# Two sets of float32 buffers for the slot weights, and a fixed order of a slot's work on TensorE, VectorE and ScalarE

## The chip, the cores and the metric

The kernel runs on one core of one Trainium2 chip. The metric is the time of one execution in microseconds (us), as the device reports it. Lower is better.

## What is computed

Three layers in a chain: linear attention, a SoLU feed-forward layer, and a top-1 routed mixture of experts.

```python
k_s = softmax(k, axis=seq); q_s = softmax(q)              # (8, 8, 576, 64)
x = q_s @ (k_s^T @ v)                                     # -> 4608 tokens x 512
h = x @ w_in                                              # 512 x 1024
x = layernorm(h * softmax(h)) * g_ln @ w_out              # 1024 x 512
e_idx = argmax(x @ w_gate + modality_bias[modality_id])   # 8 experts
for e in range(8):                                        # w1 512 x 1024, w2 1024 x 512, float32
    mask = e_idx == e
    out[mask] = gate_w[mask] * (relu(x[mask] @ w1[e]) @ w2[e])
```

All inputs are float32. Products of float32 are made as three float16 products (high by high, high by low, low by high), so each weight is split into a high and a low part at a scale that is a power of two.

## The kernel before

**Stages.** First come the attention sums, then 36 tiles of 128 tokens pass through attention and the SoLU layer (the tile stage, lines 480 to 820; `ph` is the first product, `lnT` the transposed activations that a DMA brings, `px` the second product). Each tile also routes its tokens. From about 544 us on the routed layer runs in slots: a slot is 256 tokens of one expert. Eighteen slots are always there (`NMIN`), the rest is done in half slots by `tail` (L1328).

**One slot.** `slot_load_w` (L929) loads the expert's weights on SP's queue: `w1` in four DMAs of 512 KB (L938) into `raw1`, `w2` in four (L941) into `raw2`. There is one such pair of float32 buffers, and from slot 1 on a load carries a condition, so that nothing is moved when the slot's expert is that of the slot before:

```python
g["kw"] = {} if i == 0 else {"cond": ld(i, 2, 1)}
SY.dma_start(out=raw1[:, c, :], in_=w1[ds(g["e"], 1), ...], **g["kw"])
```

`slot_split` (L948) makes the float16 pairs `w1b[i % 2]` and `w2b[i % 2]`: `mx` takes maxima of `w1` on DVE (L956, four), `l1` row sums of `w2` on ACT (L960, four, whose other output goes into a part of `w2b` that is written later). `fin` (L963) makes the scales from them: exponents on DVE (L102, L103), diagonals `dg` (L113), a product `pm` on PE (L115), a maximum `p2m` over it (L117), the scale `sc` (L123) and its inverse (L125, L967). Then `sp1` and `sp2` write the high part on ACT (L149) and the low part on DVE (L156), four pieces each for `w1b` and `w2b`.

`slot_gather` (L997) fetches the slot's tokens: their indices `six` (L1004, a small DMA on SP), two gathers of 128 rows into `sg` (L1009, issued by POOL), and two DMA transposes into `sxt` (L1013, on SP).

`slot_mm` (L1069) computes: `st1` on PE, two halves of 48 products `sph` (L1090); `ev1` after each half, `rl` and the high part of `hh` on ACT (L1097, L1098), the low part on DVE (L1099); `st2`, two halves of 24 products `spo` (L1108); `ev2` on ACT, `ob` (L1119), and a scatter of 128 rows to the output (L1022, issued by POOL).

**What sets the order.** Work is put into a queue by `at(time, fn)` (L64), and `flush` emits it in order of these times, which the loop at L1318 writes out by hand. `behind` (L70) holds a piece back behind a marked instruction, and `ordered` (L1062) keeps PE's products in the order of emission. For the rest a list scheduler (`TC_KW`, L37), which works from a cost model, orders the instructions of each engine. The loop body for slot i:

```python
mm(i, b)
if i:
    slot_gather(i + 1, b + 0.5)
    split(i + 1, b)
slot_load_w(i + 2, b + 18.0, 0.01)
```

So while PE does slot i, the weights of slot i + 1 are measured, scaled and split, and the load for slot i + 2 follows.

Of the kernel before, what the change touches and what calls it, by code (L numbers as in the profile page):

```python
# [43 lines left out]
def tile_attn_moe_moe(ctx, tc, q, kT, v, w_in, w_out, g_ln, mod, w_gate, bias, w1, w2, out):  # L44
# [884 lines left out]
    def slot_load_w(i, time, dt):  # L929
        g = {}  # L930

        def regs():
            g["e"] = ld(i, 1, NE - 1)
            g["kw"] = {} if i == 0 else {"cond": ld(i, 2, 1)}

        def one(r, c):
            if r == 1:
                SY.dma_start(out=raw1[:, c, :], in_=w1[ds(g["e"], 1), c * 128:(c + 1) * 128, :].rearrange(  # L938
                    "o p f -> (o p) f"), **g["kw"])
            else:  # L940
# [127 lines left out]

    def slot_mm(i, times):  # L1069
# [5 lines left out]
        def st1(k):  # L1075
            ordered(st1_, k)

        def st2(k):
            ordered(st2_, k)

        def st1_(k):
# [3 lines left out]
            for ff in range(4):  # L1085
                f = 4 * k + ff
                n = 0
                for c in range(4):
# [4 lines left out]

        def ev1(k):
# [3 lines left out]
            A.activation(out=g["hh"][:, 0, sl, :], in_=rl, func=AF.Copy)  # L1098
            V.tensor_tensor(out=g["hh"][:, 1, sl, :], in0=rl, in1=g["hh"][:, 0, sl, :], op=ALU.subtract)  # L1099

        def st2_(k):
            if k == 0:
# [2 lines left out]
            for h in range(2):
                for f in range(4 * k, 4 * k + 4):
                    for a, b2 in ((0, 0), (0, 1), (1, 0)):
                        last_mm[:] = [T.matmul(po[:, h, :], hh[:, a, f, h * 128:(h + 1) * 128], s2[:, b2, f, 0:DM],  # L1108
                                               start=(f == 0 and (a, b2) == (0, 0)), stop=(f == 7 and a == 1))]
# [7 lines left out]
        def ev2(h):  # L1117
# [1 line left out]
            A.activation(out=ob, in_=g["po"][:, h, :], func=AF.Copy, scale=g["rs"][:, h:h + 1])  # L1119
# [268 lines left out]
```

## Time and profile before

| | |
|---|---|
| time, median of 3 runs | 995.01 us (992.31 to 995.11) |
| the profiled execution | 994.26 us |
| its span, first to last instruction | 992.5 us |
| mean granted clock of TensorE | 0.968 |
| PE busy | 871.6 us (88%) |
| DVE, ACT, POOL busy | 779.0 (78%), 696.8 (70%), 475.5 (48%) us |
| DMA, mean over the span | 135 GB/s |

The profile is of one execution. PE is TensorE, DVE VectorE, ACT ScalarE, POOL GpSimd, SP the engine whose queue issues most DMAs. Busy times are sums over the whole span; the stages differ. A wait stands in square brackets behind an instruction, with what released it. A transfer's issue has a row on the queue's engine; the transfer itself is seen only in the DMA share and in who waits for it.

### The profile page before, as it was taken

To read this page: it belongs to the slowest core of one execution; us is meant where nothing else is said; L and a number is where in the kernel's file an instruction comes from. 1 tells how busy PE (TensorE), PEld (TensorE's weight loads), DVE (VectorE), ACT (ScalarE), POOL (GpSimd) and SP (SyncE) were. 2 spreads that over 40 slices of the span, in tenths; PEclk is the share of its full clock that TensorE was granted. 3 is DMA by queue.
4 is the path that set the end of the run, shared out by engine and by line. 5 is a ranking of instruction groups with operands and counts; after the bars stand their busy time and mean duration, and the time that the engine had idled before them with its cause. 6 is when DMAs were issued, how large, how long until landed. Compare 5 with 4: busy or idle time off the path is not lost.

```text
span 992.5 us, 18881 instructions
## 1 busy us (share of the span) xinstructions
PE 871.6 (88%) x6566; PEld 584.8 (59%) x6566; DVE 779.0 (78%) x1591; ACT 696.8 (70%) x1041; POOL 475.5 (48%) x892
## 2 busy tenths in 40 slices
PE   2476898999999998999996989999998999999983
PEld 1244666667676665766765755666665566666552
DVE  6979687887888868886897588888887877778871
ACT  5568677777876867675783657777768777777771
POOL 6734568777787776665656331222322222222221
PEclk9977999999999999999997998999999999999997
DMA  9959969787978687677445332222263223332360
GB/s 313 310 128 194 231 142 192 162 172 148 203 156 184 143 159 192 138 188 185 83 107 108 70 78 55 66 65 65 76 195 115 65 65 79 81 78 65 102 198 25
DMA packets 247483, 133.52 MB, mean 135 GB/s; under 512 B 215441, under 2 KB 218065, under 8 KB 247378
## 3 DMA queue, kind: packets, MB, share of 16 engines
q1 hardware_dynamic: 239938, 112.20, 50.3%
q0 software_dynamic: 7152, 20.01, 6.5%
q8 instruction: 53, 0.87, 0.4%
q14 instruction: 52, 0.43, 0.1%
q10 hardware_dynamic: 288, 0.02, 0.0%
HBM read 130.94 MB, written 19.86 MB: 152 GB/s over the span
## 4 chain that ended last, share of the span: by engine, by line
DVE 39%; PE 21%; issue 11%; ACT 10%; DMA 9%; POOL 7%; SPq 1%; ACTq 0%; POOLq 0%; DVEq 0%
PE spo L1108 9%; DVE w1b L156 8%; DVE w2b L156 7%; DVE smm L956 6%; PE px L710 4%; PE ph L596 3%; ACT w1b L149 2%; DVE vhl L156 2%; PE sph L1090 2%; DVE hh L1099 2%; DVE zhl L648 2%; ACT e L619 2%; DMA raw<-in_v_dram 2%; DVE t L625 1%; PE pk L502 1%
## 5 line engine op out<-in xcount | busy, mean ns | idle before, releaser
L710 PE MATMUL px<-w2b,lnT 128*128 128x256 f16 x1728 | 207.6, 277 | 12.2 <-DMA lnT<-zhl 12.2
L1090 PE MATMUL sph<-sxt,w1b 128*128 128x256 f16 x1728 | 199.3, 274 | 14.3 <-DVE w1b L156 11.5
L1108 PE MATMUL spo<-w2b,hh 128*128 128x512 f16 x864 | 194.6, 379 | 11.6 <-DVE hh L1099 9.8
L596 PE MATMUL ph<-w1b,xTt 128*128 128x512 f16 x864 | 198.6, 384 | 3.0 <-ACT xTt L149 3.0
L1090 PEld LDWEIGHTS <-w1b 128*128 128x128 f16 x1728 | 166.9, 98 | 47.5 <-DVE w1b L156 20.7
L710 PEld LDWEIGHTS <-lnT 128*128 128x128 f16 x1728 | 167.8, 99 | 40.0 <-DMA lnT<-zhl 13.2
L1108 PEld LDWEIGHTS <-hh 128*128 128x128 f16 x864 | 82.7, 98 | 112.8 <-DVE hh L1099 18.4
L596 PEld LDWEIGHTS <-xTt 128*128 128x128 f16 x864 | 84.4, 99 | 97.7 <-issue 5.1
L1022 POOL DMA_INDIRECT out_dram<-ob,six x37 | 59.1, 1597 | 151.3 <-ACT ob L1119 141.5
L149 ACT ACTIVATE w1b<-raw,sc 128x1024 f16<-128x1024 f32 x76 | 81.2, 1137 | 63.3 <-DVE sc L123 63.3
L156 DVE SCALAR_TENSOR_TENSOR w1b<-raw,sc,w1b 128x1024 f16<-128x1024 f32 x76 | 93.0, 1279 | 15.9 <-ACT w1b L149 15.9
L156 DVE SCALAR_TENSOR_TENSOR w2b<-raw,sc,w2b 128x1024 f16<-128x1024 f32 x76 | 95.3, 1275 | 0.0
L956 DVE TENSOR_REDUCE smm<-raw 128x1 f32<-128x1024 f32 x76 | 91.8, 1210 | 0.9 <-DMA raw<-in_moe_w_dram 0.9
L1009 POOL DMA_INDIRECT sg<-xs_scr,six x38 | 37.7, 991 | 107.3 <-issue 77.3
L960 ACT ACTIVATE w2b<-raw 128x1024 f16<-128x1024 f32 x76 | 79.4, 1046 | 7.9 <-DMA raw<-in_moe_w_dram 7.9
L149 ACT ACTIVATE w2b<-raw,sc 128x1024 f16<-128x1024 f32 x76 | 81.0, 1134 | 0.0
L648 DVE TENSOR_TENSOR zhl<-e,zhl 128x1024 f16<-128x1024 f32 x36 | 59.8, 1664 | 17.9 <-ACT zhl L645 15.1
L630 ACT ACTIVATE e<-t,hts 128x1024 f32<-128x1024 f32 x36 | 41.2, 1145 | 25.6 <-DVE t L625 25.4
L619 ACT ACTIVATE e<-ph,hnm,ghb 128x1024 f32<-128x1024 f32 x32 | 38.4, 1200 | 26.8 <-DVE hnm L615 23.7
L530 POOL TENSOR_TENSOR qr<-qr,qmx 128x512 f32<-128x512 f32 x36 | 38.9, 1084 | 33.2 <-DVE qmx L529 24.4
L643 ACT ACTIVATE e<-t,hna,ha 128x1024 f32<-128x1024 f32 x36 | 44.3, 1232 | 14.7 <-DVE hna L640 7.1
L625 DVE SCALAR_TENSOR_TENSOR t<-ph,ghb,e 128x1024 f32<-128x1024 f32 x32 | 41.0, 1281 | 15.1 <-ACT e L619 14.9
(263 smaller groups left out, 1434.6 us busy)
## 6 DMA issues: line engine op xcount, KB each, us to landing
raw<-in_moe_w_dram SPq DMA_DIRECT2D x160, 512.0 KB
qr<-in_q_dram SPq DMA_DIRECT2D x36, 256.0 KB
xs_scr<-xrows SPq DMA_DIRECT2D x17, 528.0 KB
kt<-in_k_dram SPq DMA_DIRECT2D x30, 288.0 KB
raw<-in_v_dram SPq DMA_DIRECT2D x8, 1024.0 KB
w1b<-in_moe_w_in_dram SPq DMA_DIRECT2D x8, 512.0 KB
w1b<-in_moe_w_out_dram SPq DMA_DIRECT2D x4, 512.0 KB
w2b<-w1b SPq DMA_DIRECT2D x4, 512.0 KB
```

The source lines that it names most:

```text
L149: return A.activation(out=hi, in_=src, func=AF.Copy, scale=scale)
L156: return e.scalar_tensor_tensor(out=lo, in0=src, scalar=scale, in1=hi, op0=ALU.mult, op1=ALU.subtract)
L596: T.matmul(ph[:, n, :], xt[:, a, c, :], w1s[:, b2, c, n * 512:(n + 1) * 512], start=(c == 0 and (a, b2) == (0, 0)), stop=(c == 3 and a == 1))
L619: mark["ea", t] = A.activation(out=g["e"], in_=big[t], func=AF.Exp, bias=g["nm"], scale=gh, accum_out=es)
L625: mark["tv", t] = V.scalar_tensor_tensor(out=g["t"], in0=big.pop(t), scalar=gn, in1=g["e"], op0=ALU.mult, op1=ALU.mult, accum_out=s)
L648: mark["zv", t] = V.tensor_tensor(out=g["z"][:, 1], in0=g["e"], in1=g["z"][:, 0], op=ALU.subtract)
L710: T.matmul(px[:, n, 0:c1 - c0], lt[:, a, f, :], w2s[:, b2, f, c0:c1], start=(f == 0 and (a, b2) == (0, 0)), stop=(f == 7 and a == 1))
L956: V.tensor_reduce(out=g["mm"][:, c:c + 1], in_=raw1[:, c, :], axis=AX.X, op=ALU.max, apply_absolute_value=True)
L960: A.activation(out=s2[:, 0, 2 * c:2 * c + 2, 0:DM], in_=raw2[:, 2 * c:2 * c + 2, :], func=AF.Abs, accum_out=g["mm"][:, 4 + c:5 + c])
L1022: x = G.indirect_dma_start(out=out, out_offset=bass.IndirectOffsetOnAxis(ap=ix, axis=0), in_=ob, in_offset=None, bounds_check=NTOK - 1, oo ...
L1090: last_mm[:] = [T.matmul(ph[:, ff, :], s1[:, a, c, f * 128:(f + 1) * 128], xt[:, 4 * b2 + c, :], start=(n == 0), stop=(n == 11))]
L1108: last_mm[:] = [T.matmul(po[:, h, :], hh[:, a, f, h * 128:(h + 1) * 128], s2[:, b2, f, 0:DM], start=(f == 0 and (a, b2) == (0, 0)), stop=( ...
```

## The change

It makes these edits:

- A second set of float32 weight buffers. Slot 0 and odd slots use `raw1`, `raw2` as before; even slots from 2 on use `raws`: the tiles `e`, `t` (for `w1`), `zhl` and `lnT` (for `w2`) of the pool `ap2`, which the tile stage has left. `l1` writes its unused output into a tile `xTt` of that pool.
- The loads lose their condition: every slot moves its 4 MB. They are put in three slots ahead; the `w1` part at b + 7.5, the `w2` part at b + 20.9 and behind the transposes of slot i + 1.
- Maxima and sums (`mx`, `l1`) and the scale are made for slot i + 2 while PE does slot i, the split for slot i + 1. `fin` is two parts, `fin1` (up to `pm`) and `fin2` (from `p2m` on); `pm` stands after 36 of the 48 `spo`.
- `chained` fixes the order of emission on PE, DVE and ACT together, for the slot's pieces from slot 1 (or 3, for the maxima) on.
- The gather of slot i + 1 is put in at b - 8 in place of b + 0.5; the lists' pads (`pad`) go later.

```diff
+    last = {}
+
+    def chained(fn, *args):
+
+
+        with ExitStack() as st:
+            for x in last.values():
+                st.enter_context(tc.issue_after(x.ins))
+            new = fn(*args)
+        last.update(new)
+    rawb = {}
+
+    def raws(i, r, c):
+
+        if i == 0 or i % 2:
+            return raw1[:, c, :] if r == 1 else raw2[:, 2 * c:2 * c + 2, :]
+        if (r, c) not in rawb:
+            n = ("e", "t", "zhl", "lnT")[2 * (r - 1) + c // 2]
+            if n in "et":
+                x = ap2.tile([128, 2, 512], F32, tag=n, name=n)
...
+                x = x.rearrange("p (a b) -> p a b", a=2)
+            rawb[r, c] = x.rearrange("p a b -> p (a b)") if r == 1 else x
+        return rawb[r, c]
...
         def regs():
             g["e"] = ld(i, 1, NE - 1)
-            g["kw"] = {} if i == 0 else {"cond": ld(i, 2, 1)}
-
         def one(r, c):
             if r == 1:
...
-            at(time + dt * n, one, 1 + n // 4, n % 4)
+            at(time + dt * n if time2 is None or n < 4 else time2 + dt * (n - 4), one, 1 + n // 4, n % 4)
...
+            if i == 0:
+                o = s2[:, 0, 2 * c:2 * c + 2, 0:DM]
+            else:
+                if "o" not in rawb:
+                    rawb["o"] = ap2.tile([128, 2, 4, 128], F16, tag="xTt", name="xTt", bufs=3)
+                o = rawb["o"].rearrange("p a b c -> p (a b c)").rearrange("p (a b) -> p a b", a=2)
+            return {"A": A.activation(out=o, in_=raws(i, 2, c), func=AF.Abs, accum_out=g["mm"][:, 4 + c:5 + c])}
...
+        def fin1():
+            m2 = small("sm2", 2, bufs=2)
...
+            dg = diagonals(exponent(m2))
+            g["pm"] = ps1.tile([128, 4, 128], F32, tag="xT", name="pm")
+            return {"V": dg[1], "T": T.matmul(g["pm"][:, 0:2, :], oneb, dg[0], start=True, stop=True)}
+
+        def fin2():
+            g["c2"], i2 = (small(n, 2, bufs=2) for n in ("sc2", "si2"))
+            r = small("p2m", 2)
+            V.tensor_reduce(out=r, in_=g["pm"][:, 0:2, :], axis=AX.X, op=ALU.max)
+            inverse(r, g["c2"], i2)
+            return {"V": V.tensor_scalar(out=sic[:, i % 4:i % 4 + 1], in0=i2[:, 0:1], scalar1=i2[:, 1:2],
+                                         scalar2=2.0 ** 19, op0=ALU.mult, op1=ALU.mult)}
...
+                if 2 < i <= NMIN:
+                    at(tm[c], chained, mx, c)
+                    at(tl[c], chained, l1, c)
+                else:
+                    with behind(*(pins[-1] + tuple((n, 1, 3) for n in (("s2a", "s2v") if i == 2 else ())))):
+                        at(tm[c], mx, c)
+                        at(tl[c], l1, c)
+                for t, f in ((t1, sp1), (t2, sp2)):
+                    if 1 < i <= NMIN:
+                        at(t[c], chained, f, c)
+                    else:
+                        at(t[c], f, c)
...
+            chained(st1_, k)
+        def st2(k, h):
+            chained(st2_, k, h)
+        def ev1(k):
+            (chained if i else free)(ev1_, k)
+        def ev2(h):
+            (chained if i else free)(ev2_, h)
...
         at(b + 5.3, ev1, 1)
-        at(b + 4.0, row_scales)
-        at(c, st2, 0)
-        at(c + 5.3, st2, 1)
-        at(d + 0.1, ev2, 0)
-        at(d + 0.2, ev2, 1)
+        at(b + 4.0 if i else a, row_scales)
+        at(c, st2, 0, 0)
+        at(c + 2.6, st2, 0, 1)
+        at(c + 5.25, st2, 1, 0)
+        at(c + 7.9, st2, 1, 1)
+        at(d - 2.1, ev2, 0)
+        at(d + 0.1, ev2, 1)
...
+    SLT = dict(l1=(7.4, 7.41, 7.42, 10.8), mx=(7.45, 7.46, 7.47, 10.85), fin=(15.8, 16.1), s1=(0.2, 0.21, 0.22, 0.23),
+               s2=(15.9, 16.0, 16.2, 16.3), ga=-8.0, ld=(7.5, 20.9))
...
-    slot_load_w(1, TE + 13.1, 0.9)
+    slot_load_w(1, TE + 8.0, 0.2)
...
-        at(TE + 32.0 + 2.0 * e, pad, e)
-
...
+    def split(i, b, d):
+
+        f = lambda n, x: [x + y for y in SLT[n]]
+        slot_split(i, (f("mx", b), f("l1", b), f("fin", b), f("s1", d), f("s2", d)))
...
-    split(1, S0 + 0.05)
+    with behind(("za", NT - 1), ("zv", NT - 1)):
+        split_(1, TE + 12.1, S0 + 1.0)
+    split_(2, S0 + 11.1, bs(1))
+    with behind(("zv", NT - 1)):
+        slot_load_w(2, S0, 0.1, S0 + 5.5)
+    slot_gather(2, S0 + 1.5)
+    with behind(("sx", 2, 1)):
+        slot_load_w(3, S0 + 12.0, 0.3)
     for i in range(NMIN):
         b = bs(i)
         mm(i, b)
-        if i:
-            slot_gather(i + 1, b + 0.5)
-            split(i + 1, b)
-        slot_load_w(i + 2, b + 18.0, 0.01)
+        if i > 1:
+            slot_gather(i + 1, b + SLT["ga"])
+        if 3 <= i + 2 <= NMIN:
+            split(i + 2, b, bs(i + 1))
+        if 4 <= i + 3 <= NMIN + 1:
+            with behind(("sx", i + 1, 1)):
+                slot_load_w(i + 3, b + SLT["ld"][0], 0.01, b + SLT["ld"][1])
```

How it moves instructions, at three places. Names are the program's; L975 and L978 of the new file are the loads of w1 and w2 (L938, L941 before), L1070 is `six` (L1004), L1079 the transposes (L1013).

SP's queue in a steady slot, before:

```order
L926 TENSOR_LOAD hsb
L1004 ISA
L1004 DMA six<-perm_scr 128x2x1
L1013 DMA_TRANSPOSE sxt_7632<-sg_7635 128x8x128
L1013 DMA_TRANSPOSE sxt_7632<-sg_7636 128x8x128
L926 TENSOR_LOAD hsb x2
L938 ISA
L938 DMA raw_95<-in_moe_w_dram 128x1024
```

and now:

```order
L975 ISA
L975 DMA t<-in_moe_w_dram 128x1024
L946 TENSOR_LOAD hsb
L1070 ISA
L1070 DMA six<-perm_scr 128x2x1
L1079 DMA_TRANSPOSE sxt_7632<-sg_7635 128x8x128
L1079 DMA_TRANSPOSE sxt_7632<-sg_7636 128x8x128
L978 ISA
L978 DMA zhl<-in_moe_w_dram 128x2x512
```

`six` and the transposes came after all eight loads of a slot. Now `six` comes right behind the four loads of `w1` and the loads of `w2` right behind the transposes.

DVE in the second half of slot 0, ahead of its second `hh` (L1099 before, L1166 now). L156 and L176 are the low part of the split, L993 is `mx`, `p2m` and the rows on it are `fin`; the other names are the routing of the last tile. Before:

```order
L965 TENSOR_REDUCE sm_8126<-smm 128x2
L102 TENSOR_SCALAR p2a<-sm_8126 128x2
L103 TENSOR_SCALAR p2b<-p2a 128x2
L113 TENSOR_SCALAR dg<-eye,p2b 128x128 x2
L773 SCALAR_TENSOR_TENSOR rpj,rpos<-pr,roh 128x8
L1099 TENSOR_TENSOR hh<-rl,hh 128x1024
L117 TENSOR_REDUCE p2m<-pm 128x2
```

and now:

```order
L176 SCALAR_TENSOR_TENSOR w1b_92<-raw_95,sc_8110,w1b_92 128x1024 x2
L766 TENSOR_REDUCE rr<-rw 128x1
L176 SCALAR_TENSOR_TENSOR w1b_92<-raw_95,sc_8110,w1b_92 128x1024 x2
L176 SCALAR_TENSOR_TENSOR w2b_94<-raw_96,sc_8110,w2b_94 128x2x512 x4
L993 TENSOR_REDUCE smm<-e 128x1
L776 TENSOR_REDUCE rgs<-rex 128x1
L993 TENSOR_REDUCE smm<-e 128x1
L993 TENSOR_REDUCE smm<-t 128x1 x2
L793 SCALAR_TENSOR_TENSOR rpj,rpos<-pr,roh 128x8
L1166 TENSOR_TENSOR hh<-rl,hh 128x1024
```

The whole split of slot 1 and the four maxima of slot 2 now stand ahead of `hh`.

SP's queue at the end of the tile stage, the transposes `lnT` of the last two tiles (L652 before, L672 now). Before:

```order
L938 ISA
L938 DMA raw_95<-in_moe_w_dram 128x1024
L1013 DMA_TRANSPOSE sxt_7631<-sg_7633 128x8x128
L652 DMA_TRANSPOSE lnT<-zhl 128x16x128
L1013 DMA_TRANSPOSE sxt_7631<-sg_7634 128x8x128
L760 DMA xs_scr<-xrows 128x2x528
L652 DMA_TRANSPOSE lnT<-zhl 128x16x128
```

and now:

```order
L1079 DMA_TRANSPOSE sxt_7631<-sg_7633 128x8x128
L975 ISA
L975 DMA raw_95<-in_moe_w_dram 128x1024
L978 ISA
L978 DMA raw_96<-in_moe_w_dram 128x2x512
L672 DMA_TRANSPOSE lnT<-zhl 128x16x128
L1079 DMA_TRANSPOSE sxt_7631<-sg_7634 128x8x128
L978 ISA
L978 DMA raw_96<-in_moe_w_dram 128x2x512
L978 ISA
```

The transposes of tile 34 and 35 were behind three loads of `w1` of slot 1. Now the fourth load of `w1` and one of `w2` come before the first of them, and the rest of `w2` before the second.

## Rows read from the trace of the kernel before

**Rows 1.** Page, part 2: DMA engines' busy share, in tenths, in 40 equal slices.

```profile
DMA  9959969787978687677445332222263223332360
```

**Rows 2.** Timeline of PE, 536 to 965: start, us, instruction, count, wait and releaser.

```profile
536.65 7.36 PE L710 MATMUL px<-w2b,lnT 128*128 128x256 f16 x48 [8.47 <-DMA lnT<-zhl]
...
570.36 10.64 PE L1090 MATMUL sph<-sxt,w1b 128*128 128x256 f16 x96
580.84 0.59 PE L1108 MATMUL spo<-w2b,hh 128*128 128x512 f16 x2
...
594.47 0.39 PE L1090 MATMUL sph<-sxt,w1b 128*128 128x256 f16 x2 [2.45 <-ACT w1b L149]
...
620.37 1.36 PE L1090 MATMUL sph<-sxt,w1b 128*128 128x256 f16 x11
...
632.59 5.35 PE L1108 MATMUL spo<-w2b,hh 128*128 128x512 f16 x24 [0.54 <-DVE hh L1099]
...
642.63 1.54 PE L1090 MATMUL sph<-sxt,w1b 128*128 128x256 f16 x11
...
733.44 1.53 PE L1090 MATMUL sph<-sxt,w1b 128*128 128x256 f16 x11
735.67 9.45 PE L1090 MATMUL sph<-sxt,w1b 128*128 128x256 f16 x85 [0.69 <-DVE w1b L156]
...
759.22 1.03 PE L1090 MATMUL sph<-sxt,w1b 128*128 128x256 f16 x8 [0.28 <-DMA sxt<-sg]
...
964.10 1.02 PE L1043 MATMUL sph<-sxt,w1b 128*128 128x128 f16 x11
```

**Rows 3.** Timeline of ACT in a steady slot.

```profile
890.73 4.27 ACT L149 ACTIVATE w1b<-raw,sc 128x1024 f16<-128x1024 f32 x4 [4.09 <-DVE sc L123]
```

**Rows 4.** Timeline of DVE: slot 0's second hh, a steady slot's w1b split.

```profile
562.16 1.23 DVE L1099 TENSOR_TENSOR hh<-rl,hh 128x1024 f16<-128x1024 f32 x1 [1.22 <-ACT hh L1098]
...
891.91 4.87 DVE L156 SCALAR_TENSOR_TENSOR w1b<-raw,sc,w1b 128x1024 f16<-128x1024 f32 x4 [0.82 <-ACT w1b L149]
```

**Rows 5.** Windows: us, busy us (count) of PE, PEld, DVE, ACT, POOL, clock, DMA share, GB/s.

```profile
443.00:449.00 6.00, 6.00 (x48) 3.64 (x46) 3.44 (x13) 4.01 (x5) 5.07 (x17) 1.00 1.02 368
595.00:605.00 10.00, 8.08 (x50) 5.41 (x51) 10.00 (x9) 9.02 (x12) 1.61 (x1) 0.66 0.12 47
733.00:747.50 14.50, 12.69 (x105) 9.76 (x104) 13.13 (x12) 10.13 (x12) 3.19 (x2) 1.00 0.96 322
882.00:904.70 22.70, 21.47 (x147) 13.96 (x146) 18.30 (x24) 17.66 (x23) 5.73 (x6) 1.00 0.30 72
886.00:893.00 7.00, 7.00 (x35) 3.23 (x33) 3.85 (x10) 2.91 (x4) 1.91 (x4) 1.00 0.72 152
893.00:901.00 8.00, 7.30 (x58) 5.32 (x56) 8.00 (x8) 7.30 (x8) 0.99 (x1) 1.00 0.01 2
901.50:905.00 3.50, 3.50 (x34) 3.13 (x33) 3.50 (x4) 3.50 (x6) 1.98 (x1) 1.00 0.42 155
```

**Rows 6.** Timeline of SP's queue: start, us the issue took, instruction, count.

```profile
441.70 8.47 SPq L652 DMA_TRANSPOSE lnT<-zhl  x1
...
526.22 0.87 SPq L938 DMA_DIRECT2D raw<-in_moe_w_dram  x3
...
531.94 2.80 SPq L652 DMA_TRANSPOSE lnT<-zhl  x1
...
744.78 0.38 SPq L1004 DMA_DIRECT2D six<-perm_scr  x1
...
882.95 0.39 SPq L1004 DMA_DIRECT2D six<-perm_scr  x1
888.71 2.82 SPq L1013 DMA_TRANSPOSE sxt<-sg  x2
```

**Rows 7.** Timeline of POOL: first gather of slot 9's rows, and of a steady slot's.

```profile
751.14 0.99 POOL L1009 DMA_INDIRECT sg<-xs_scr,six  x1 [8.81 <-issue]
...
885.39 0.99 POOL L1009 DMA_INDIRECT sg<-xs_scr,six  x1 [4.58 <-issue]
```

More of the change, by code (lines that the diff above doesn't have):

```diff
@@ L112, in over_partitions @@
         for i in range(n):
-            V.tensor_scalar(out=dg[:, i, :], in0=eye, scalar1=t[:, i:i + 1], scalar2=None, op0=ALU.mult)
+            x = V.tensor_scalar(out=dg[:, i, :], in0=eye, scalar1=t[:, i:i + 1], scalar2=None, op0=ALU.mult)
+        return dg[:, 0:n, :], x
+    def over_partitions(t):
+        n = t.shape[-1]
+        dg, _ = diagonals(t)
         pm = ps1.tile([128, 4, 128], F32, tag="xT", name="pm")
-        T.matmul(pm[:, 0:n, :], oneb, dg[:, 0:n, :], start=True, stop=True)
+        T.matmul(pm[:, 0:n, :], oneb, dg, start=True, stop=True)
         r = small("p2m", n)
@@ L963, in fin @@
-        def fin():
-            m2, g["c2"], i2 = (small(n, 2, bufs=2) for n in ("sm2", "sc2", "si2"))
-            V.tensor_reduce(out=m2, in_=g["mm"].rearrange("p (a b) -> p a b", a=2), axis=AX.X, op=ALU.max)
-            pow2(m2, g["c2"], i2)
-            V.tensor_scalar(out=sic[:, i % 4:i % 4 + 1], in0=i2[:, 0:1], scalar1=i2[:, 1:2], scalar2=2.0 ** 19,
-                            op0=ALU.mult, op1=ALU.mult)
+            if "mm" not in g:
+                g["mm"] = small("smm", 8, bufs=2)
+            if i == 0:
[4 more added lines that the diff above has]
+                o = rawb["o"].rearrange("p a b c -> p (a b c)").rearrange("p (a b) -> p a b", a=2)
@@ L993, in slot_split @@
                     at(tt_(tiles[c]) + 12.1, sp2, c)
-        at(tf, fin)
+        for t, f in zip(tf, (fin1, fin2)):
+            if 2 < i <= NMIN:
+                at(t, chained, f)
+            else:
+                at(t, f)
         slot_w[i] = (s1, s2)
@@ L1012, in tr @@
         def tr(h):
-            SY.dma_start_transpose(out=xt[:, :, h * 128:(h + 1) * 128], in_=gr[h][:, 0:512].bitcast(F16))
+            mark["sx", i, h] = SY.dma_start_transpose(out=xt[:, :, h * 128:(h + 1) * 128], in_=gr[h][:, 0:512].bitcast(F16))
         at(time, idx)
@@ L1097, in ev1, with st2_ @@
             A.activation(out=rl, in_=g.pop(("ph", k)), func=AF.Relu, scale=2.0 ** -19)
[L1098 to L1102, printed above, removed]
+            x = A.activation(out=g["hh"][:, 0, sl, :], in_=rl, func=AF.Copy)
+            y = V.tensor_tensor(out=g["hh"][:, 1, sl, :], in0=rl, in1=g["hh"][:, 0, sl, :], op=ALU.subtract)
+            return {"A": x, "V": y}
+        def st2_(k, h):
+            if (k, h) == (0, 0):
                 g["po"] = psb.tile([128, 2, 512], F32, tag="big", name="spo")
             hh, po = g["hh"], g["po"]
[L1105 to L1109, printed above, removed]
+            for f in range(4 * k, 4 * k + 4):
+                for a, b2 in ((0, 0), (0, 1), (1, 0)):
+                    x = T.matmul(po[:, h, :], hh[:, a, f, h * 128:(h + 1) * 128], s2[:, b2, f, 0:DM],
+                                 start=(f == 0 and (a, b2) == (0, 0)), stop=(f == 7 and a == 1))
+            return {"T": x}
         def row_scales():
@@ L1115, in row_scales, with ev2_ @@
                                 scalar1=sic[:, i % 4:i % 4 + 1], scalar2=None, op0=ALU.mult)
[L1117 removed]
+        def ev2_(h):
             ob = pb.tile([128, DM], F32, tag="ob", name="ob", bufs=4)
[L1119 removed]
+            x = A.activation(out=ob, in_=g["po"][:, h, :], func=AF.Copy, scale=g["rs"][:, h:h + 1])
             scatter(ob, ix[:, h:h + 1])
+            return {"A": x}
         a, b, c, d = times
```

74 lines of the change are left out of this document (35 added, 39 removed).

## The prediction

> **What bounds the kernel now.** I read the page's slices first, to see which stage has which limit. In the stage of the slots (the last 18 or so of the 40 slices) the DMA engines stand at two or three tenths [rows 1], while PE is busy for 21.47 of a slot's 22.70 us [rows 5]. The high slices there are slots in which weights really arrive; elsewhere the load of an unchanged expert is skipped.
>
> Then TensorE's timeline [rows 2], from first sph to first sph. A steady slot takes 22.70 us (642.63 to 733.44 is four of them). Two waits stand in it: 0.69 for DVE's last w1b part, after 11 matmuls, and 0.54 for DVE's hh. Without waits, 96 sph take 10.48 (570.36 to 580.84), 46 spo with pm 10.04 (632.59 to 642.63), and two more spo at 10.04/46 add 0.44: 20.96. So waits and restarts cost 1.74 a slot. Slots 3 to 17 take 343.73 (620.37 to 964.10), slot 8 of them 25.78 (733.44 to 759.22), because weights arrive in it and sxt comes late.
>
> Where the waits come from is seen on ACT and DVE [rows 3, 4]. Maxima, pm, scale, split and use of one slot's weights all stand within the slot before it: ACT idles 4.09 for DVE's scale, and the split (4.27 of ACT, 4.87 of DVE for w1) ends only as PE needs it. Neither engine is full: 17.66 and 18.30 of 22.70 [rows 5].
>
> **The change part by part.** *Steady slots, engines.* The scale is now made two slots ahead and the split one slot ahead, so the 0.69 and the 0.54 should go: 20.96 if nothing else comes. DVE and ACT issue the same instructions as before, so their 18.30 and 17.66 still fit. The l1 output in another tile and the split of fin into two cost nothing: same instructions, covered by PE. So does pm's move to after 36 spo.
>
> *Steady slots, DMA.* The loads lose their condition, so each slot really moves 4.19 MB (8 chunks of 0.524). This lies beside PE, but not beside everything. On SP's queue a slot is now: w1, six, two transposes of the next slot's rows, w2 (the order above). Six stands behind four w1 chunks, w2 behind the transposes, so they form a ring:
> - six to the first gather: 2.44 with idle DMA (882.95 to 885.39) [rows 6, 7]. Behind w1 the time counts from when the chunks have drained: in slot 8 six was issued at 744.78, data ran until 747.5, and the gather came at 751.14 [rows 5 to 7]. That is 6.36 instead of 2.44, or 3.6 after the drain.
> - gather to transposes: 3.32 (885.39 to 888.71).
> - transposes to the end of their data: 4.29 (888.71 to 893.0; the DMA then rests until 901, share 0.01) [rows 5, 6].
>
> With the 2.44 these make 10.05 in which no weights move. The chunks lie between two bounds. From below: 368 GB/s while slot 0's load ran [rows 5] is 1.42 a chunk, 11.40 for eight. From above: slot 8's load, 14.5 at share 0.96, less the scatters (3.5 x 0.42 = 1.47, both [rows 5]), leaves 12.45, or 1.56 a chunk. I take 1.42, since that row shows chunks following one another without an issue that waits; and of the scatters' 1.47 I count half, 0.7, because one of the two can fall where six or a gather is under way. The ring is 10.05 + 11.40 + 0.70 = 22.15, more than PE's 20.96: DMA becomes the bound. Its ends are 10.05 + 11.40 = 21.45 and, with 3.6 for 2.44, slow chunks and all scatters, 11.21 + 12.45 + 1.47 = 25.13. Fifteen slots: 343.73 - 15 x 22.15 = **11.5 saved** (29.3 at PE's 20.96; 22 saved at 21.45; 33 lost at 25.13).
>
> The Trainium skill, "DMA: Bandwidth & Descriptors", Specifications, gives a core about 358 GB/s from HBM: an estimate of 1.46 a chunk, 22.45 for the ring and 993 in all. The 368 of this trace lies above it, so I keep the row.
>
> *Start of the slots.* Slot 1's load was skipped before (3 issues in 0.87 at 526.22 [rows 6]); now it moves data ahead of lnT of tile 34 (five chunks before it) and lnT of tile 35 (three more), on the same queue. Before, slot 0's load did this once: a lnT transpose behind 7 chunks was held 8.47 [rows 6], against 2.80 at 531.94. PE already waits 8.47 for lnT of tile 34 at 536.65 [rows 2]. The gather of slot 0 covers part; five chunks from 526.2 at 1.5 end near 534 instead of letting lnT start at 531.94, and the transpose itself shares with them: **+4** (none if the gathers hide it, +10 if both lnT are held 8.5).
>
> *Slot 0.* In its second half DVE now has w1b x4, w2b x4 (the splits of slot 1) and four maxima of slot 2 ahead of hh. Before, hh ran at 562.16 after a wait of 1.22 for ACT alone [rows 4]. Now three sets of four passes stand there, 3 x 4.87 = 14.6 if each is like the w1b row, and the maxima wait for slot 2's w1. Some 6 to 7 of it fits between PE's first and second half of sph (5.2 and its hh); **8** is new, and PE waits for it with spo. In return slots 1 and 2 lose their waits for w1b (2.45 at 594.47 and smaller ones behind it [rows 2]): 24.11 and 25.90 become 21 and 21.6, 7.4 less. Net **+0.6**. After the 2.45 wait the granted clock was 0.66 on the mean of 10 us, between the levels of 1.2 and 2.4 GHz [rows 5]: 10 x 0.34 = 3.4 of lost PE time. A wait of 8 brings at least that again: I add **+2**, since part of it falls on the wait itself (bounds 0 and 5).
>
> *End and the rest.* The tail's first wait is of the slots' kind and goes: **-0.7**. The pads move to a later place on SP, in slot 1; I cost them at nothing, since PE waits for none of them, and at one issue each (six takes 0.39 [rows 6]) if they held up the queue there. POOL's queue has scatters and gathers in one row; at 5.73 of 22.70 [rows 5] a gather waits there only if the scatter ahead has a late ob.
>
> **The sum.** 994.26 (the profiled run; its span is 992.5) + 4 + 0.6 + 2 - 11.5 - 0.7 = **988.7**. The profiled run lies 0.75 under the median of 995.01, so the change is about -0.6%. In general the time is 656.4 + 15 x ring, and no change comes at a ring of 22.6.
>
> **The rivals.**
> - **B: the loads keep up and PE is the bound.** 994.26 + 5.9 - 29.3 = 971; with 0.4 of waits left in each slot, 977. For it: the DMA engines' work in a slot is 8 x 1.42 + 7.0 x 0.72 [rows 5] + 1.47 = 17.9, under 20.96. Against it: six and w1 share a queue, and 744.78 to 751.14 shows that the small load does wait. The Trainium skill, "Trainium Kernel Development and Optimization", Best Practices, has this as a rule: double-buffer, so that DMA overlaps compute. By that rule the second set alone would bring B; the 6.36 of slot 8 speaks against it here. Chance 0.13.
> - **C: the ring is as slow as in slot 8.** The mechanism is the order of SP's queue: six behind w1, w2 behind the transposes. It decides from a ring of 22.8 on, that is, 12.75 for chunks and scatters (370 GB/s with the scatters' 0.52 MB, where slot 8's window has 322 [rows 5]). At 12.45 + 1.47 with 2.44: 23.97, time 1016; with a third of the scatters hidden, 1008. On ACT, l1 then waits for w2's data, and by the fixed order rl and hh are queued behind them and PE behind these. For it: the only slot in the rows that shows loads beside a slot's work is this one. Against it: there w2's issue waited for w2b on DVE, which the second set removes. Chance 0.28.
> - **D: a tie.** The ring is 22.4 to 22.8, or the start costs 8 more than I count: 992 to 998. That the loads are not really issued early, because a mark or an order holds them, ends here too. Chance 0.19.
> - My case, a ring of 21.5 to 22.4: 979 to 992. Chance 0.40.
>
> **How the numbers follow.** A difference of 0.3% (3 us) is about what a measurement of this kernel can tell from none. Faster by more: my case and B, 0.53. The same: D, 0.19. Slower: C, 0.28. The range leaves out the fast part of B below 969 and the part of C above 1007: 969 to 1007. My own case alone would be 979 to 992.
>
> **What will show it.** In the profile after: first sph to first sph of 22.15 in slots 4 to 16, with the wait on sxt (transposes) or, behind l1, on hh, and no wait on w1b. The slices of the slots' stage show DMA at eight or nine tenths and about 200 GB/s. On SP, six to gather of 4 to 6, then 3.3, then 4.3. PE waits about 8 in slot 0 for hh, some 12 for lnT of tile 34, and shows a clock near 0.5 behind them. I am wrong if a slot is PE-bound (20.96, no wait longer than 0.3), if sxt is never waited for, or if the start costs over 15.

## The result

| | before | after |
|---|---|---|
| median | 995.06 us (4 runs) | 1009.91 us (1007.23 to 1011.92, 4 runs) |
| profiled execution, its span | 994.26, 992.5 us | 1009.4, 1007.7 us |
| mean granted clock | 0.968 | 0.954 |
| ratio, 95% interval | | 1.0148 (1.011 to 1.0185) |

The change made the kernel slower by 1.5%. That is rival C, by its mechanism too; the time lies 3 us above the range.

### The profile after

The page's slices, TensorE's granted clock and the DMA engines' busy share in tenths (before: [rows 1]).

```profile
PEclk9977999999999998999996989999989999999997
DMA  9959979777977677786539797887787888777750
```

The DMA engines now stand at seven or eight tenths in the slots' stage, where it was two or three: every load is real.

PE's timeline (answers to [rows 2]): the last tiles, slots 0, 1 and 3, two slots in the middle, the tail.

```profile
524.55 5.48 PE L730 MATMUL px<-w2b,lnT 128*128 128x256 f16 x48
543.38 0.17 PE L786 MATMUL pr<-roh,tri 128*128 128x8 f16 x1 [13.34 <-POOL roh L769]
...
544.17 8.07 PE L730 MATMUL px<-w2b,lnT 128*128 128x256 f16 x48 [0.28 <-DMA lnT<-zhl]
552.08 5.40 PE L1156 MATMUL sph<-sxt,w1b 128*128 128x256 f16 x48
...
578.03 0.17 PE L786 MATMUL pr<-roh,tri 128*128 128x8 f16 x1 [4.64 <-POOL roh L769]
...
582.50 0.19 PE L817 MATMUL pc<-cum,ones 128*128 128x8 f16 x1 [3.41 <-DVE rpj L793]
...
590.17 10.64 PE L1156 MATMUL sph<-sxt,w1b 128*128 128x256 f16 x96
...
632.07 8.13 PE L1156 MATMUL sph<-sxt,w1b 128*128 128x256 f16 x73
...
699.27 10.64 PE L1156 MATMUL sph<-sxt,w1b 128*128 128x256 f16 x96
...
716.27 0.60 PE L1175 MATMUL spo<-w2b,hh 128*128 128x512 f16 x2 [1.17 <-ACT hh L1165]
717.53 2.33 PE L1175 MATMUL spo<-w2b,hh 128*128 128x512 f16 x10 [0.65 <-DVE hh L1166]
...
722.48 10.64 PE L1156 MATMUL sph<-sxt,w1b 128*128 128x256 f16 x96
...
741.83 1.04 PE L1175 MATMUL spo<-w2b,hh 128*128 128x512 f16 x2 [3.53 <-ACT hh L1165]
743.10 4.45 PE L1175 MATMUL spo<-w2b,hh 128*128 128x512 f16 x10 [0.23 <-DVE hh L1166]
...
750.10 5.08 PE L1156 MATMUL sph<-sxt,w1b 128*128 128x256 f16 x45
...
980.79 5.52 PE L1109 MATMUL sph<-sxt,w1b 128*128 128x128 f16 x96
```

From these first sph the time is split as in the prediction, with the same points of before beside it:

| stretch | before | after | difference | predicted |
|---|---|---|---|---|
| up to px of tile 33 | 522.70 | 524.55 | +1.9 | 0 |
| px of tile 33 to slot 0 | 21.27 | 27.53 | +6.3 | +4 |
| slots 0 to 2 | 76.40 | 79.99 | +3.6 | +2.6 |
| slots 3 to 17 | 343.73 | 348.72 | +5.0 | -11.5 |
| tail | 28.40 | 26.91 | -1.5 | -0.7 |
| span | 992.5 | 1007.7 | +15.2 | -5.6 |

The wait for w1b has gone from the slots, as the edit meant. In its place PE waits in the second product for hh, first for ACT's half (1.17 and 3.53 in the rows), then for DVE's. Behind the wait of 3.53, ten spo took 4.45, where the same ten took 2.33 a slot earlier.

Why hh is late stands on ACT (slot of 699.27). l1, on the rows as `xTt<-`, waits for w2's data, and the second half's rl and hh are queued behind it.

```profile
705.88 1.06 ACT L1165 ACTIVATE hh<-rl 128x1024 f16<-128x1024 f32 x1
710.31 1.06 ACT L1005 ACTIVATE xTt<-zhl 128x1024 f16<-128x1024 f32 x1 [3.38 <-DMA zhl<-in_moe_w_dram]
...
714.12 1.00 ACT L1164 ACTIVATE rl<-sph 128x1024 f32<-128x1024 f32 x1
715.16 1.06 ACT L1165 ACTIVATE hh<-rl 128x1024 f16<-128x1024 f32 x1
```

Why w2's data are late stands on SP's queue and POOL's, over one turn (answers to [rows 6, 7]; the first row of POOL belongs to the start of slot 0).

```profile
700.97 2.94 SPq L1079 DMA_TRANSPOSE sxt<-sg  x2
704.16 1.71 SPq L978 DMA_DIRECT2D zhl<-in_moe_w_dram  x2
706.12 1.32 SPq L978 DMA_DIRECT2D lnT<-in_moe_w_dram  x2
708.01 2.46 SPq L975 DMA_DIRECT2D raw<-in_moe_w_dram  x4
711.08 0.38 SPq L1070 DMA_DIRECT2D six<-perm_scr  x1
725.44 4.63 SPq L1079 DMA_TRANSPOSE sxt<-sg  x2
```

```profile
535.51 0.29 POOL L1182 TENSOR_SCALAR srs<-sg,sic 128x1 f32<-128x1 f32 x1 [3.31 <-DMA sg<-xs_scr,six]
...
721.49 1.53 POOL L1075 DMA_INDIRECT sg<-xs_scr,six  x1 [14.33 <-issue]
723.33 1.75 POOL L1075 DMA_INDIRECT sg<-xs_scr,six  x1 [0.30 <-issue]
```

Windows: us, busy us (count) of PE, PEld, DVE, ACT, POOL, granted clock, DMA share, GB/s (answers to [rows 5]). A packet counts where it starts, so a share can come out over 1.

```profile
699.27:722.48 23.21, 21.39 (x146) 14.02 (x145) 18.21 (x23) 17.99 (x22) 7.96 (x6) 1.00 0.81 250
710.00:718.00 8.00, 6.18 (x29) 2.48 (x28) 3.35 (x4) 7.20 (x11) 0.00 (x0) 1.00 1.04 405
719.00:723.00 4.00, 4.00 (x22) 2.03 (x21) 3.79 (x11) 2.68 (x4) 1.51 (x1) 1.00 0.02 7
740.00:747.50 7.50, 5.44 (x13) 1.77 (x14) 5.48 (x9) 6.95 (x8) 1.51 (x1) 0.54 0.61 236
```

Read them as one turn. The transposes are issued at 700.97, the four loads of w2 and the four of w1 right behind them, six at 711.08. On SP's queue nothing there waits for PE, and for DVE at most 0.5 at a time. The data run until about 718.5. Then the DMA engines stand still (share 0.02 from 719 to 723): six lands, the gathers start at 721.49, the transposes at 725.44, and only behind these the next w2. That turn is 24.47 us long (700.97 to 725.44); the mean of 14 turns, from the transposes at 632.52 to those at 962.08, is 23.54. The engines that compute are not the bound, and the DMA engines rest for part of each turn.

### The profile page after: what moved, and what is told of

Same layout as the page of the kernel before. It is cut to its first block, busy times and chain, and to the rows that moved or that the text cites. A ratio compares the mean times of both kernels' runs of the same rounds, so it can differ in the third digit from the quotient of the medians.

```text
span 1007.7 us, 18872 instructions
## 1 busy us (share of the span) xinstructions
PE 874.8 (87%) x6566; PEld 588.6 (58%) x6566; DVE 776.3 (77%) x1591; ACT 702.2 (70%) x1041; POOL 518.5 (51%) x892
## 4 chain that ended last, share of the span: by engine, by line
DVE 31%; DMA 19%; ACT 14%; issue 13%; PE 11%; POOL 9%; SPq 2%; POOLq 0%; DVEq 0%; ACTq 0%
DVE w1b L176 6%; DVE w2b L176 4%; DMA lnT<-in_moe_w_dram 4%; DMA raw<-in_moe_w_dram 4%; PE ph L616 3%; DVE smm L993 2%; DVE vhl L176 2%; PE sph L1156 2%; DMA six<-perm_scr 2%; PE spo L1175 2%; DMA xs_scr<-xrows 2%; DVE zhl L668 2%; DMA sg<-xs_scr,six 2%; DVE hh L1166 2%; DVE t L645 2%
## 5 line engine op out<-in xcount | busy, mean ns | idle before, releaser
L1175 PE MATMUL spo<-w2b,hh 128*128 128x512 f16 x864 | 204.3, 390 | 24.6 <-ACT hh L1165 15.8
L1156 PE MATMUL sph<-sxt,w1b 128*128 128x256 f16 x1728 | 191.7, 273 | 0.0
L1075 POOL DMA_INDIRECT sg<-xs_scr,six x38 | 47.9, 1261 | 225.7 <-issue 112.8
L1175 PEld LDWEIGHTS <-hh 128*128 128x128 f16 x864 | 83.9, 100 | 133.5 <-ACT hh L1165 21.7
L1166 DVE TENSOR_TENSOR hh<-rl,hh 128x1024 f16<-128x1024 f32 x36 | 44.3, 1230 | 70.6 <-ACT hh L1165 70.4
L1088 POOL DMA_INDIRECT out_dram<-ob,six x37 | 56.4, 1525 | 56.3 <-ACT ob L1187 42.3
L668 DVE TENSOR_TENSOR zhl<-e,zhl 128x1024 f16<-128x1024 f32 x36 | 59.7, 1659 | 16.5 <-ACT zhl L665 14.7
L1005 ACT ACTIVATE xTt<-raw 128x1024 f16<-128x1024 f32 x36 | 37.9, 1052 | 36.8 <-DMA raw<-in_moe_w_dram 36.6
L176 DVE SCALAR_TENSOR_TENSOR w1b<-raw,sc,w1b 128x1024 f16<-128x1024 f32 x40 | 49.0, 1281 | 5.1 <-ACT w1b L169 5.1
L663 ACT ACTIVATE e<-t,hna,ha 128x1024 f32<-128x1024 f32 x36 | 44.3, 1231 | 11.5 <-DVE hna L660 7.5
L1187 ACT ACTIVATE ob<-spo,srs 128x512 f32<-128x512 f32 x36 | 22.8, 683 | 40.8 <-issue 30.0
L570 POOL TENSOR_TENSOR qhl<-qr,qhl 128x512 f16<-128x512 f32 x36 | 45.6, 1268 | 9.5 <-ACT qhl L566 9.4
L176 DVE SCALAR_TENSOR_TENSOR w2b<-raw,sc,w2b 128x1024 f16<-128x1024 f32 x40 | 49.5, 1279 | 0.0
```

What stands on the lines that cost most here:

```text
L176: return e.scalar_tensor_tensor(out=lo, in0=src, scalar=scale, in1=hi, op0=ALU.mult, op1=ALU.subtract)
L570: G.tensor_tensor(out=g["hl"][:, 1], in0=qf, in1=g["hl"][:, 0], op=ALU.subtract)
L663: A.activation(out=g["e"], in_=g["t"], func=AF.Identity, bias=g["na"], scale=g["a"])
L668: mark["zv", t] = V.tensor_tensor(out=g["z"][:, 1], in0=g["e"], in1=g["z"][:, 0], op=ALU.subtract)
L1075: G.indirect_dma_start(out=gr[h], out_offset=None, in_=xs, in_offset=bass.IndirectOffsetOnAxis(ap=ix[:, h:h + 1], axis=0))
L1088: x = G.indirect_dma_start(out=out, out_offset=bass.IndirectOffsetOnAxis(ap=ix, axis=0), in_=ob, in_offset=None, bounds_check=NTOK - 1, oo ...
```

## The experiments

Four explanations were held against each other: the **ring** (six, gather, transposes and chunks follow one another on one queue), **bandwidth** (too many bytes for 21 us, in whatever order), the **reader** (l1 stands too early on ACT), and, for the start, **collision** (the first real loads) against **order** (what stands ahead on DVE). Each ratio is to the kernel before, timed in the same rounds on the same chip. Experiments 1 to 5, the kernels named skip_all and start_order ran on three chips, so across these groups the ratios compare, not the times.

### 1. six a turn earlier

```diff
-        at(time, idx)
+        at(time - (14.0 if 5 <= i <= NMIN else 0.0), idx)
```

with the loads from slot 6 on held behind the six that now precedes them.

> The changed kernel with one thing moved: from slot 5 on the small load of the indices (six) is issued one turn earlier on SP's queue, so that it no longer stands between the loads of w1 and the gathers of the same turn. Ring theory (six, gather, transposes and the eight chunks follow one another, 23.5 us a turn): a turn loses the 2.1 from the drained queue to the gather and the 3.9 from gather to transposes, the ring falls to about 18.6, PE becomes the bound with 21.0 to 21.6 a slot, 973 to 988 us in all. Bandwidth theory (the DMA engines simply have too much to move in 21 us, whatever the order): slots stay at 23 to 23.5, 1006 to 1013 us.

Measured: 979.32 us, ratio 0.9842 (0.9809 to 0.9874). PE's timeline of one slot, the window of that slot, and the queues of SP and POOL:

```profile
784.60 10.64 PE L1163 MATMUL sph<-sxt,w1b 128*128 128x256 f16 x96
795.08 7.93 PE L1182 MATMUL spo<-w2b,hh 128*128 128x512 f16 x36
...
805.55 1.69 PE L1163 MATMUL sph<-sxt,w1b 128*128 128x256 f16 x14
```

```profile
784.60:805.55 20.95, 20.95 (x146) 14.19 (x145) 18.35 (x24) 17.88 (x22) 5.69 (x6) 1.00 0.90 275
```

```profile
793.04 0.38 SPq L1076 DMA_DIRECT2D six<-perm_scr  x1
795.27 2.92 SPq L1086 DMA_TRANSPOSE sxt<-sg  x2
```

```profile
799.03 1.04 POOL L1082 DMA_INDIRECT sg<-xs_scr,six  x1 [9.21 <-DMA six<-perm_scr]
```

Slots 4 to 17 take 20.95 each (the last 20.84), with no wait from one first sph to the next. The same 4.19 MB move, at share 0.90 and 275 GB/s. Its six, issued at 793.04, still stands behind chunks, and the gather at 799.03 still waits for it; but the transposes at 795.27 are those of the turn before, whose rows lay ready, and the rows of 799.03 are not wanted until the next transposes at 816.22. Six and gather have left the ring, and w2's loads follow the transposes without them. SP's queue now waits for DVE to have split the w2 that it is to overwrite (73.1 us in 40 waits from 658 to 952), so the loads have time to spare. So bandwidth is not the limit at 21 us; the place of one small load is. Slots 2 and 3, which the edit comes too late for, took 22.3 and 25.0 (one expectation below calls them 3 and 4).

### 2. Loads skipped where the buffers already hold the expert

```diff
-        tt(hsb[:, 2, K:], e[:, K:], e[:, L:N - 1], ALU.not_equal)
+        tt(hsb[:, 2, K + 1:], e[:, K + 1:], e[:, L:N - 2], ALU.not_equal)
...
+            g["kw"] = {"cond": ld(i, 2, 1)} if NPICK < i <= NMIN + 1 else {}
...
```

> The changed kernel, but from slot 6 on a load is skipped when the slot two before had the same expert (its weights are then still in that set of buffers). Ring and bandwidth theory alike: the slots without loads fall to 20.95 to 21.3, about 12 of 15, 975 to 988 us. If instead the new order on ACT and DVE is what costs time, slots stay over 22 without loads too, and the time over 995. It measures what the second set and the fixed order give when nothing has to be loaded, against the 22.70 a slot of the kernel before.

Measured: 977.92 us, ratio 0.9831 (0.9800 to 0.9861). Slots without a load take 20.95; two of the 15, at 632.68 and 738.86, take 22.38 and 22.78. The new order itself is worth what the prediction said (20.96): 20.95 against 22.70 a slot.

### 3. l1 behind the second hh

```diff
-    SLT = dict(l1=(7.4, 7.41, 7.42, 10.8), ...
+    SLT = dict(l1=(10.8, 10.81, 10.82, 10.83), ...
```

> The changed kernel with all four l1 on ACT behind the second half's hh, where three of the four stood ahead of it. Reader theory (w2's data are only some 3 us later than their readers are placed, and the readers hold up hh): the wait of PE for hh goes and slots take 21 to 21.5, 973 to 988 us. Ring theory: the ring does not hang on l1, so slots stay at 23 to 23.5 on the mean and PE waits for sxt or for a later part instead, 1000 to 1013 us.

Measured: 1014.97 us, ratio 1.0192 (1.0153 to 1.0231). PE and ACT in one slot:

```profile
795.22 0.27 PE L1012 MATMUL pm<-dg,oneb 128*128 128x256 bf16 x1 [3.35 <-DVE dg L123]
```

```profile
785.20 1.06 ACT L1165 ACTIVATE hh<-rl 128x1024 f16<-128x1024 f32 x1
788.89 1.06 ACT L1005 ACTIVATE xTt<-raw 128x1024 f16<-128x1024 f32 x1 [2.63 <-DMA raw<-in_moe_w_dram]
```

hh is on time, and the wait has moved to pm, whose diagonals need l1's sums: 27.8 us in 12 waits from 630 to 985. Moving the readers alone wins nothing; the data come when the ring brings them. Slots 3 to 17 take 23.6 on the mean, and the time lies 2 us above the ring theory's range. What PE waits for here is a later part, which the expectation left open, not sxt.

### 4. The kernel before, with every load real

```diff
-            g["kw"] = {} if i == 0 else {"cond": ld(i, 2, 1)}
+            g["kw"] = {}
```

> The kernel before with its loads made unconditional, one set of buffers, no other edit. Ring theory: one turn is longer than 23.5, since with a single set w2's loads wait for the split as well; each slot takes about 25.8, as slot 8 did in the kernel before, so 16 slots at 3.1 more: 1035 to 1055 us. Bandwidth theory: 23 to 23.5 a slot as in the changed kernel, 1003 to 1010 us.

Measured: 1037.27 us, ratio 1.0431 (1.0395 to 1.0468). Slots 4 to 16 take 24.9 on the mean (659.02 to 982.99), a little under the 25.8. Waits of PE from 630 to 980: us in total, times, longest.

```profile
PE spo L1108 <- ACT hh L1098: 16.7, 14, 2.5
PE spo L1108 <- DVE hh L1099: 15.3, 24, 1.4
```

The loads of w2 do wait for the split here, as expected: SP's queue waits 92.5 us in 56 waits for DVE's w2b in the same stretch. This run parts the change into two. Real loads alone cost 42 us (995 to 1037); the second set, the depth and the fixed order take 27 of these back (1037 to 1010).

### 5. The start, with loads

Four kernels on top of six_early. six_late1 puts slot 1's load behind slot 0's transposes:

```diff
-    slot_load_w(1, TE + 8.0, 0.2)
+    with behind(("sx", 0, 1), ("lt", NT - 2)):
+        slot_load_w(1, TE + 12.0, 0.2)
```

> The kernel of six_early (979 us), with the load of slot 1 put behind slot 0's second transpose and the lnT transpose of tile 34. Collision theory (the real load of slot 1 slows slot 0's gather; POOL waits for the gathered rows, and the routing of the last tiles is queued behind it; PE's queue waits for the routing): first sph of slot 0 comes back from 552.5 to 544 to 546, POOL's wait for sg from 3.3 to under 1. Slot 0 gets longer by 0 to 6, as slot 1's weights come later; 970 to 979 us. If the start was lost to the order of the queues alone and not to the collision, first sph stays over 549.

six_hh_first holds slot 2's maxima and sums behind slot 0's second hh (`more = (("hh", 0, 1),) if i == 2 else ()` among their marks). six_both has both edits, six_both_slot4 also the early six from slot 4 on.

Of six_hh_first:

> The kernel of six_early, with slot 2's four maxima and sums held back behind slot 0's second hh. Order theory: the routing's row (rpj) and hh come 4.8 earlier on DVE, PE's two waits in slot 0 (3.4 and 0.95) go, slot 0 falls from 38.2 to 33 to 35, 974 to 977 us. If the clock or the routing on POOL sets slot 0, it stays over 37.

Of six_both:

> Both edits at once: if they add, first sph of slot 0 at 544 to 546 and slot 0 at 30 to 35, 964 to 973 us. If slot 1's weights are then what hh waits for on DVE (the whole split of slot 1 stands ahead of it), the gain of the start is given back in slot 0, 973 to 979 us.

Of six_both_slot4:

> Both edits, and the early six from slot 4 on instead of slot 5, with the pads 8 us earlier so that they still come first. Ring theory: slots 3 and 4, which took 22.3 and 25.0 in six_early, fall to 21 to 22.5, 2 to 5 us less than six_both. If the pads, which wait for the table of slots, now hold up SP's queue, slot 2 or 3 gets longer by as much.

| run | time, ratio (interval) | first sph of slot 0 | slots 0, 1, 2 |
|---|---|---|---|
| six_early | 979.32, 0.9842 (0.9809 to 0.9874) | 552.53 | 38.18, 20.95, 22.29 |
| six_late1 | 987.43, 0.9906 (0.9884 to 0.9927) | 547.40 | 41.77, 24.20, 25.40 |
| six_hh_first | 982.88, 0.9863 (0.9841 to 0.9884) | 551.88 | 34.36, 25.17, 20.95 |
| six_both | 982.85, 0.9869 (0.9843 to 0.9895) | 546.35 | 43.31, 22.98, 25.70 |
| six_both_slot4 | 985.46, 0.9885 (0.9864 to 0.9907) | 548.72 | 41.53, 29.87, 22.01 |

Each edit did what it said at its place, and none won time: six_late1 is slower than six_early, and the intervals of the other three overlap with its interval. A later load brings slot 0's start back by 5 (POOL's wait for the rows falls from 3.3 to 0.47), and slots 0 to 2 take 10 longer. In slot 0 it is not slot 1's split that comes late: it starts on DVE at 565.1, where six_early has 565.2. Slot 2's w2 does. Its l1 stands ahead of hh on ACT, and PE waits for hh:

```profile
577.78 1.06 ACT L1011 ACTIVATE xTt<-zhl 128x1024 f16<-128x1024 f32 x1 [4.48 <-DMA zhl<-in_moe_w_dram]
```

```profile
579.93 1.03 PE L1182 MATMUL spo<-w2b,hh 128*128 128x512 f16 x2 [7.03 <-ACT hh L1172]
```

hh first shortens slot 0 by 3.8, and slot 1 gets 4.2 longer. An early six for slot 4 shortened slot 2 (22.01 against 25.70), and slot 1 lost more (29.87 against 22.98). Of these expectations the totals were missed throughout.

### 6. The start, without loads

skip_all extends the condition of experiment 2 to slot 1 and slots 3 to 5, so that of these first slots slot 2 alone loads; skip_all_hh adds hh first, skip_all_six the early six. start_order is skip_all_six with slot 1's maxima behind slot 0's first hh and slot 2's behind its second.

Of skip_all:

> As skip (978 us), but slots 1 and 3 to 5 too load only when the buffers hold another expert; of the first slots slot 2 alone moves data. Load theory of the start: what cost 11.7 us up to slot 3 is that the weights of slots 1 to 3 really move there, whatever the order; first sph of slot 0 at 544 to 546, slots 0 to 2 together 64 to 72 us (80.0 in the changed kernel, 76.4 before), 960 to 969 us. Order theory of the start (slot 2's maxima ahead of hh, the early row scales on POOL): first sph stays over 549 and slot 0 over 36, 973 to 979 us.

Of skip_all_hh:

> skip_all with slot 2's maxima behind slot 0's second hh. In six_hh_first this gave slot 0 4 us and took them back in slot 1, where the next weights then came late. If that was the work of the start being one queue of loads, here, with one real load, the gain stays: 2 to 5 us less than skip_all. If it is taken back here too, the same time as skip_all within 1.5 us, and DVE's own work is the limit of slots 0 and 1.

Of skip_all_six:

> skip_all with the early six of six_early. Ring theory: it matters only around the two changes of expert, where skip had two slots of 22.4 and 22.8: 1 to 3.5 us less than skip_all, with all slots from 5 on at 20.95. If those slots are long for another reason (a late l1 or split), no difference.

Of start_order:

> skip_all_six (971.6 us) with the order of DVE at the start as it was in the kernel before: slot 1's maxima behind slot 0's first hh, and slot 2's behind its second, which the planner then also puts ahead of slot 1's split. If DVE's order there is what lengthens slot 0 (40 us in skip_all_six without any load of slots 1, 3 and 4, against 26.4 in the kernel before), slot 0 falls to 26 to 30 and slots 0 to 2 together from 81.9 to 70 to 78 us, 960 to 968 us. If it only moves the wait into slots 1 and 2, slots 0 to 2 stay at 79 to 82 and the time within 3 us of skip_all_six.

| run | time, ratio (interval) | px of tile 33 to slot 0 | slots 0, 1, 2 |
|---|---|---|---|
| skip_all | 974.47, 0.9788 (0.9759 to 0.9818) | 21.69 | 40.03, 20.95, 20.95 |
| skip_all_hh | 972.85, 0.9775 (0.9738 to 0.9812) | 21.50 | 36.29, 22.05, 20.95 |
| skip_all_six | 971.61, 0.9770 (0.9742 to 0.9797) | 21.84 | 40.03, 20.95, 20.95 |
| start_order | 979.62, 0.9831 (0.9793 to 0.9868) | 21.50 | 34.40, 33.71, 20.95 |

PE of skip_all, and POOL's wait for slot 0's first gathered rows there and in the kernel before:

```profile
526.31 5.48 PE L730 MATMUL px<-w2b,lnT 128*128 128x256 f16 x48
540.95 7.09 PE L730 MATMUL px<-w2b,lnT 128*128 128x256 f16 x48 [9.16 <-DMA lnT<-zhl]
...
548.00 5.40 PE L1158 MATMUL sph<-sxt,w1b 128*128 128x256 f16 x48
...
581.21 6.66 PE L1177 MATMUL spo<-w2b,hh 128*128 128x512 f16 x21 [4.41 <-DVE rgs L777]
...
588.03 10.64 PE L1158 MATMUL sph<-sxt,w1b 128*128 128x256 f16 x96
```

```profile
534.43 0.29 POOL L1184 TENSOR_SCALAR srs<-sg,sic 128x1 f32<-128x1 f32 x1 [0.42 <-DMA sg<-xs_scr,six]
```

```profile
530.63 0.29 POOL L1114 TENSOR_SCALAR srs<-sg,sic 128x1 f32<-128x1 f32 x1 [0.27 <-DMA sg<-xs_scr,six]
```

Without slot 1's load the stretch up to slot 0 is back at 21.7 (21.27 before, 27.53 after), and POOL waits 0.42 for the rows and not 3.31. That part of the start is the collision, shown. The place of the load seems to count too: in experiment 4 slot 1's load is real as well, but three of its chunks and not five stand ahead of lnT of tile 34, and the stretch is 23.67. No run tested that by itself. Slot 0 stays at 40 without any load of slots 1, 3 and 4, so these loads do not make it long; the order does in part. In skip_all_hh slot 0 falls by 3.7 and slot 1 takes 1.1 of it back. There the slot of the change of expert is 3.4 longer (26.21 at 728.02, against 22.83), and the total, 1.6 less, lies between its two forecasts. In start_order slot 0 falls to 34.4, but the wait moves into slot 1:

```profile
580.43 11.90 PE L1166 MATMUL sph<-sxt,w1b 128*128 128x256 f16 x96
...
599.52 1.04 PE L1186 MATMUL spo<-w2b,hh 128*128 128x512 f16 x2 [7.07 <-ACT hh L1175]
...
614.14 6.06 PE L1166 MATMUL sph<-sxt,w1b 128*128 128x256 f16 x54
```

Both of start_order's forecasts were missed: slots 0 to 2 take 89.1 together, and at a ratio of 0.9831 against skip_all_six's 0.9770 it is some 6 us slower, not within 3. The early six did what was expected around the change of expert: skip_all's one slot of 22.83 is gone, and none over 20.95 is left from slot 1 on. For the total of skip_all the load theory was too hopeful by 5 us, since it gave slots 0 to 2 back as well; 974.47 lies in the order theory's range.

## Why the prediction was wrong

**The ring was right as a mechanism, and too short.** The failed step is the sum of 22.15 a turn, and in it the term of 12.10 for eight chunks and half the scatters; 23.54 a turn was measured. From the transposes to the drained queue a turn takes about 17.5 on the mean; less the 4.29 up to the end of the transposes' data, 13.3 are left where 12.10 was written. That is most of the 1.39. From gather to transposes it was 3.9, not 3.32 (the second gather comes 1.7 behind the first, before 1.29). From the drained queue to the gather it was 2.1, not 2.44.

The chunks by themselves were not slow. From 710 to 718, alone on the engines, they ran at 405 GB/s: by estimate 1.29 each (0.524 MB at that rate), under the 1.42 written. The stretch before is what the sum had wrong. There the scatters move beside the transposes and the first chunks, and from 702 to 710 the engines are full (share 1.00) at 233 GB/s. My choice of half the scatters alone decided the sign: with all of their 1.47 the ring is 22.92, and by the prediction's own formula, 656.4 + 15 x ring, a ring of 22.6 was the point of no change.

Two of the things to look for came out otherwise. Six was issued 10.4 ahead of its gather (711.08 to 721.49), not 4 to 6. And PE never waited for sxt in these slots, which the prediction had named as a sign of being wrong. PE's waits are those for hh behind l1, which it had named beside sxt.

**Slots 3 to 17 took 23.25 and not 22.15**: 16.5 of the 20.7 us between forecast and profiled time. Slot 3 starts ahead of the ring and takes 21.27; the others but the last wait for it. Behind a wait of over 3 us the clock was low: 0.54 on the mean of 740 to 747.5, near the lower of its two levels, 1.2 GHz. The two slots with such a wait took 27.62 and 26.46, but the slots right behind them 22.48 and 22.34, so the mean stays with the ring.

**The start was mis-sized by 4.1**, 8.1 instead of 4 (1.9 of it lie before px of tile 33, which starts between 522.5 and 526.3 in the kernels of this study, and are not explained). That lnT of tile 34 would come late was right: px waited for it until 544.17, 19.6 behind px of tile 33, against 13.95 before. What I missed is what held it. Slot 0's gather shared the DMA engines with the load. The transpose of the gathered rows stands ahead of lnT on SP's queue, which waited 6.3 for them (3.4 before). POOL waited 3.31 for them at the row scales (0.27 before), and the routing of the last tiles was queued behind. PE's row names that routing, 13.34 at 543.38, because it stands ahead of px; lnT came 0.8 later still.

**Slot 0 and after.** Slot 0 went from 26.39 to 38.09, 11.7 where 8 was written. On DVE hh did come late behind splits and maxima, and with it the routing's rpj just ahead of it, for which PE waited 3.41 at 582.50. But PE first waited 4.64 at 578.03 for a routing row of POOL, which the sum did not have. Slots 1 and 2 gave back 8.1 (7.4 written). Of the three edits to slot 0's order, six_hh_first and start_order gave all of its gain back in slot 1 or more; skip_all_hh kept 2.6 of 3.7. What sets a lower limit for slots 0 to 2 together, 79.3 in the best run here against 76.4 before, is open.

**The steady engines** were right: 20.95 without loads, and no wait on w1b. **Bandwidth**: the Trainium skill, "DMA: Bandwidth & Descriptors", Specifications, has a limit of some 358 GB/s for a core from HBM, as half of a stack's 716 for two cores. Here one core ran alone, and from 710 to 718 it moved 405; the measurement decides. The Trainium skill, "Trainium Kernel Development and Optimization", Best Practices, has double-buffering as the way to overlap DMA with compute. The second set as built here did not hide the loads (23.25 a slot); from slot 4 on in six_early they were hidden (20.95), after one small load and its gather had left the ring.

## What to carry to other kernels

Here two sets of buffers hid the loads only once nothing that the next turn needs stood behind them on their queue. So look for the small transfer, issue it and what follows from it a turn early, and see whether the same bytes then fit. When a change makes a skipped load real, price the load by the slowest row that shows it beside the other work, and cost the change against a kernel in which the load is real too. The version to keep here is the changed kernel with the early six (979.3, ratio 0.984; it makes every load, so it does not hang on the order of experts), or with skipped loads as well (971.6, ratio 0.977; it gains where a slot has the expert of the slot two before). Other orders of experts were not run.

## What was not expected of the hardware

Eight microseconds of loads from one queue ran at 405 GB/s, faster than the two windows that the prediction had (368 and 322). In six_early the DMA engines were busy for 0.90 of a slot while PE never waited, so a high share by itself was no sign of a bound; in the changed kernel the share was lower (0.81) and PE waited.
